# Nine tokens to a partition for k and v, batch 0's q in two transfers, and one batch's q transposed by DMA, in a fused attention and mixer kernel

## The chip, the cores and the metric

The kernel runs on one core of one Trainium2 chip. The metric is the device time of one execution in microseconds (us), start to end. Engines are named as in the profile: PE is TensorE, PEld its weight loads, DVE VectorE, ACT ScalarE, POOL GpSimd, SP the engine that issues most transfers. PEclk is the TensorE clock that was granted, as a share of full speed. The profile is one execution; the times beside it are several executions.

## The reference, cut to what matters

Cosine-reweighted linear attention, then a mixer over tokens with a rank-32 map, then a two-layer MLP, for 8 batches of 576 tokens with 8 heads of 64.

```python
def phi(x, c, s):                      # c, s: cos and sin of pi/2 * pos / 576
    r = np.maximum(x, 0.0)
    return np.concatenate([r * c, r * s], axis=-1)
q_p, k_p = phi(q, cos_w, sin_w), phi(k, cos_w, sin_w)
kv  = einsum('bhsf,bhsd->bhfd', k_p, v)          # 128 x 64 per head
den = einsum('bhsf,bhf->bhs', q_p, k_p.sum(2)) + 1e-6
x   = einsum('bhsf,bhfd->bhsd', q_p, kv) / den   # then heads side by side: 576 x 512
u   = x + (x.transpose(0, 2, 1) @ U @ V).transpose(0, 2, 1)   # U: 576 x 32, V: 32 x 576
out = u + np.maximum(u @ w_ch1, 0.0) @ w_ch2     # 512 -> 2048 -> 512
```

## The kernel before

576 tokens are four times 128 and a rest of 64. The kernel loads four tokens to a partition for 512 of them and the other 64 as a "tail" on 64 partitions; even batches have their tail on partitions 0 to 63, odd ones on 64 to 127. `q_tlT` holds the transposed q tails.

```python
def tail(b):
    lo = TS * (b % 2)                  # TS = 64
    return slice(lo, lo + TS)
...
q_tl = const.tile([P, H, 2 * D], BF16)
q_tlT = const.tile([P, H, P], BF16)
...
def kv_unit(b, hg, tag, bufs, eng=None):         # four heads: 5 matmuls each
    ...
            for c in range(5):
                nc.tensor.matmul(out=acc[:, i, :],
                    lhsT=k_p[b][:, c, h, :] if c < 4 else k_tl[:, h, :],
                    rhs=vx[:, c, h, :], start=(c == 0), stop=(c == 4))
...
def qtr_dma(b, c0, c1):
    ...                                          # c0 = 4: the tail
            nc.sync.dma_start_transpose(
                out=q_tlT[:, :, tail(b)],
                in_=q_tl[tail(b), :, :].rearrange("p h f -> p (h f)"))
...
def qT_of(b, c, h):
    return q_pT[b][:, c, h, :] if c < 4 else q_tlT[:, h, :]
```

The TensorE program is one long row of slots, each a group of MLP matmuls (`g1` is the first layer, `o` the second). The attention of batches 2 to 7 is laid between them at places that a table fixes: the place of kv, then, relative to it, v's and k's and q's preparation, the transposes (`None`: on TensorE; a number: by DMA), `A`, `u`, and the loads of k, v and q of the next batch. Batches 0 and 1 have a hand-written order, since their data has only just been loaded.

```python
ORD = (4, 0, 1, 2, 3)                  # tail first
PLAN = {
    2: (40, (-21, 1, G_), (-14, VV), (-14, VA), None, 14, 17, (-20, -15, -7)),
    3: (58, (-18, 1, A_), (-8, AA), (-13, VA), -11, 15, 18, (-14, 7, 8)),
    ...
}
...
    for n, c in enumerate(ORD if qtr is None else range(5)):
        put(4 + 2 * n, x_unit, c, "X", 1)
```

## Time and profile before

| | before |
|---|---|
| time, median of 3 | 321.14 us (320.8 to 322.12) |
| span in the profile | 319.6 us, clock 1.00 |
| PE, DVE, ACT busy | 97%, 48%, 47% |
| first first-layer matmul | 23.25 us |
| batch 1's kv, whole run | about 36.0 us |
| first tail group of the first layer (`gt`) | 66.82 us |
| batch 2's A | 91.97 us |

The last four rows are places in the program. The lines on which the reading of this kernel rests stand in the prediction below.

### The profile page before, as it was taken

How to read it: one execution, taken by the hardware profiler on the slowest of the kernel's cores; microseconds unless marked ns; L12 is line 12 of the kernel's file. 1: busy time of each engine (PE TensorE's matmuls, PEld its weight loads, DVE VectorE, ACT ScalarE, POOL GpSimd, SP SyncE). 2: the span in 40 equal slices, each digit the busy share in tenths (PEclk: the TensorE clock that was granted, in tenths of full speed). 3: DMA queues.
4: the chain of work that ended last, by engine and by line, in shares of the span. 5: the costliest groups of instructions: out<-in, count | busy, mean ns of one | idle time of the engine just before them, and what ended most of it. 6: DMA issues, size and time to landing. Idle time of an engine off the chain costs nothing.

```text
span 319.6 us, 5754 instructions
## 1 busy us (share of the span) xinstructions
PE 309.3 (97%) x2359; PEld 162.4 (51%) x2386; DVE 154.3 (48%) x341; ACT 150.5 (47%) x251; POOL 34.7 (11%) x71
## 2 busy tenths in 40 slices
PE   8899799999999999999999999999999999999996
PEld 2565464475545544475455444565454444464443
DVE  5866753762777646036926585154836520001211
ACT  3856756685904256658500077558400166750000
POOL 2132500300120140000211100000121100000000
PEclk9999999999999999999999999999999999999999
DMA  7999999999199927990799959940692140001122
GB/s 207 289 267 258 207 192 285 271 266 264 43 199 164 305 89 141 216 283 19 164 194 282 282 117 176 293 126 23 133 212 71 60 98 0 2 0 68 66 83 81
DMA packets 83755, 51.90 MB, mean 162 GB/s; under 512 B 51890, under 2 KB 80946, under 8 KB 83730
## 3 DMA queue, kind: packets, MB, share of 16 engines
q1 hardware_dynamic: 77154, 40.21, 54.2%
q0 software_dynamic: 6432, 11.27, 14.8%
q8 instruction: 18, 0.29, 0.4%
q10 hardware_dynamic: 144, 0.07, 0.1%
q14 instruction: 7, 0.06, 0.1%
HBM read 36.86 MB, written 9.44 MB: 145 GB/s over the span
## 4 chain that ended last, share of the span: by engine, by line
PE 86%; DMA 7%; SPq 2%; ACT 2%; issue 1%; DVE 1%; DVEq 0%
PE o_ps L545 39%; PE g_ps L493 33%; DMA kt<-in_k_dram 5%; PE gt_ps L513 4%; PE kv_ps L271 3%; PE x_ps L365 3%; PE va_ps L409 2%; DMA vst<-in_v_dram 2%; SPq L81 1%; PE a_ps L392 1%; ACT k_p L237 1%; PE t_ps L288 1%; SPq L75 1%; ACT hid L502 0%; PE d_ps L330 0%
## 5 line engine op out<-in xcount | busy, mean ns | idle before, releaser
L502 ACT ACTIVATE hid<-g_ps 128x512 bf16<-128x512 f32 x128 | 76.2, 596 | 101.1 <-PE g_ps L493 100.6
L493 PE MATMUL g_ps<-uT,w_bf 128*128 128x512 bf16 x512 | 118.5, 379 | 0.5 <-DMA w_bf<-in_moe_w_ch_dram 0.4
L545 PE MATMUL o_ps<-w_bf,hid 128*128 128x512 bf16 (+2 forms) x510 | 117.3, 372 | 1.0
L493 PEld LDWEIGHTS <-w_bf 128*128 128x128 bf16 x512 | 48.8, 98 | 56.4 <-issue 0.6
L545 PEld LDWEIGHTS <-hid 128*128 128x128 bf16 x528 | 48.6, 98 | 52.8 <-issue 1.7
L555 DVE TENSOR_TENSOR o_sb<-u_bf,o_ps 128x512 f32<-128x512 bf16 (+2 forms) x33 | 22.1, 669 | 62.7 <-PE o_ps L545 62.6
L565 POOL DMA_DIRECT2D out_dram<-o_sb x24 | 13.5, 564 | 162.6 <-DVE o_sb L555 152.5
L410 DVE TENSOR_TENSOR u_bf<-x_bf,va_ps 128x512 bf16<-128x512 bf16 x32 | 21.8, 686 | 10.1 <-PE va_ps L409 9.7
L105 DVE CAST kv<-kv_ps 128x260 bf16<-128x260 f32 x14 | 6.0, 429 | 32.2 <-PE kv_ps L271 32.2
L237 ACT ACTIVATE q_p<-qst,sinw 128x512 bf16<-128x512 f32 x22 | 15.1, 713 | 5.7 <-DMA qst<-in_q_dram 5.7
L375 DVE TENSOR_TENSOR x_bf<-x_ps,rec 128x512 bf16<-128x512 f32 x24 | 16.6, 692 | 0.8
L513 PE MATMUL gt_ps<-uT_tl,w_bf 128*128 128x128 bf16 x256 | 15.6, 219 | 0.0
L513 PEld LDWEIGHTS <-w_bf 128*128 128x128 bf16 x256 | 14.6, 98 | 0.5
L545 PE MATMUL o_ps<-w_bf,hid_tl 128*128 128x512 bf16 x61 | 14.6, 379 | 0.2
L322 DVE TENSOR_SCALAR rec<-x_ps 128x8 f32<-128x8 f32 (+1 forms) x30 | 5.0, 165 | 20.2 <-PE x_ps L365 20.1
L409 PE MATMUL va_ps<-A_sb,V_bf 128*128 128x512 bf16 x38 | 14.4, 379 | 0.0
L271 PEld LDWEIGHTS <-k_p 128*128 128x128 bf16 x256 | 11.3, 97 | 5.4 <-ACT k_p L237 1.9
L179 PE MATMUL w_ps<-zero 128*128 128x512 bf16 x38 | 12.2, 457 | 1.9 <-DVE halfpi L142 1.2
L271 PE MATMUL kv_ps<-v_ext,k_p 128*128 128x65 bf16 x256 | 12.2, 193 | 1.5 <-ACT k_p L237 0.8
L239 DVE TENSOR_SCALAR k_p<-kst,cosw 128x512 bf16<-128x512 f32 x27 | 12.9, 497 | 0.0
L103 ACT ACTIVATE v_ext<-vst 128x512 bf16<-128x512 f32 (+2 forms) x19 | 12.3, 661 | 1.0 <-DMA vst<-in_v_dram 0.9
L239 DVE TENSOR_SCALAR q_p<-qst,cosw 128x512 bf16<-128x512 f32 x24 | 11.1, 479 | 2.6 <-DMA qst<-in_q_dram 2.6
(105 smaller groups left out, 247.4 us busy)
## 6 DMA issues: line engine op xcount, KB each, us to landing
qst<-in_q_dram SPq DMA_DIRECT2D x8, 1024.0 KB, 10.4
kst<-in_k_dram SPq DMA_DIRECT2D x8, 1024.0 KB, 8.6
vst<-in_v_dram SPq DMA_DIRECT2D x6, 1024.0 KB, 10.6
out_dram<-o_sb POOLq DMA_DIRECT2D x24, 256.0 KB, 4.3
w_bf<-in_moe_w_ch_dram POOLq DMA_DIRECT2D x8, 512.0 KB, 10.9
vst<-in_v_dram SPq DMA_DIRECT2D x4, 512.0 KB, 8.5
out_dram<-o_sb SPq DMA_DIRECT2D x7, 256.0 KB, 2.3
qt<-in_q_dram SPq DMA_DIRECT2D x8, 128.0 KB, 10.4
```

Source lines behind the costliest of these rows:

```text
L237: nc.scalar.activation(out=o, in_=i, func=AF.Relu, bias=0.0, scale=w)
L239: eng.tensor_scalar(out=o, in0=i, scalar1=0.0, scalar2=w, op0=ALU.max, op1=ALU.mult)
L271: nc.tensor.matmul(out=acc[:, i, :], lhsT=k_p[b][:, c, h, :] if c < 4 else k_tl[:, h, :], rhs=vx[:, c, h, :], start=(c == 0), stop=(c == 4),)
L375: nc.vector.tensor_tensor(out=x_of(b, c, rows).rearrange("p (g i d) -> p g i d", g=2, d=D), in0=view[:, :, :, 0:D], in1=rec[rows].unsqueez ...
L409: nc.tensor.matmul(out=va, lhsT=V_bf[:, c, :], rhs=A_sb[b], start=True, stop=True)
L410: nc.vector.tensor_tensor(out=u_bf[b][:, c, :] if c < 4 else u_tl[b // 2][rows, :], in0=x_of(b, c, rows), in1=va[rows, :], op=ALU.add,)
L493: nc.tensor.matmul(out=g_ps.rearrange("p (c t) -> p c t", c=4), lhsT=w1_bf[:, d, j * P : j * P + P], rhs=uT[b][:, :, d, :], start=(d == 0) ...
L502: nc.scalar.activation(out=hid[b][:, j, :], in_=g_ps, func=AF.Relu, bias=0.0, scale=1.0)
L513: nc.tensor.matmul(out=g_ps[:, jj, :], lhsT=w1_bf[:, d, j * P : j * P + P], rhs=uT_tl[pr][:, d, :], start=(d == 0), stop=(d == 3),)
L545: nc.tensor.matmul(out=o[:, cols], lhsT=lhs[:, j, c * P : c * P + P], rhs=w2_bf[:, j, cols], start=(j == 0), stop=(j == NJ - 1),)
L555: nc.vector.tensor_tensor(out=o_sb[:, cols], in0=u[:, cols], in1=o[:, cols], op=ALU.add)
L565: eng.dma_start(out=out[b, 0:512, cols].rearrange("(p c) n -> p c n", c=4)[:, c, :], in_=o_sb[:, cols],)
```

## The change

Its intent is fewer and larger packets and no partial tiles. k and v come with nine consecutive tokens on a partition, so that 64 partitions hold a head and 128 a pair of heads; their tails vanish, and kv becomes 72 matmuls on 64 rows, even and odd head side by side in the two halves of the array. Batch 0's q comes in two transfers ahead of k. Batch 2's q is transposed by DMA as in the later batches.

```diff
+    def load_nine(dst, src, b, g0=0, g1=4, eng=None):
+        (eng or nc.sync).dma_start(
+            out=dst[:, g0:g1, :, :].rearrange("p g c d -> p g (c d)"),
+            in_=src[b].rearrange("(g hh) (p c) d -> (hh p) g (c d)", hh=2, c=9)[:, g0:g1, :],
+        )
...
-    load_main(qst[0], q, 0)
+    load_main(qst[0], q, 0, 0, 4)
+    load_main(qst[0], q, 0, 4, 8)
+    load_nine(kst[0], k, 0)
     load_tail(qt[0], q, 0)
-    load_main(kst[0], k, 0)
-    load_tail(kt[0], k, 0)
...
+        for g in range(g0, g1):
+            for c in range(9):
+                for hh in range(2):
+                    rows = slice(hh * TS, hh * TS + TS)
+                    nc.tensor.matmul(
+                        out=acc[:, hh, (g - g0) * E : (g - g0) * E + E],
+                        lhsT=k_p[b][rows, c, g, :],
+                        rhs=v_ext[b % 2][rows, g, c, :],
+                        start=(c == 0),
+                        stop=(c == 8),
+                    )
...
-            lo = c % 4 * R
+            lo = c % 4 * R if b > 0 else 0        # batch 0's A on 32 rows
...
-        2: (40, (-21, 1, G_), (-14, VV), (-14, VA), None, 14, 17, (-20, -15, -7)),
+        2: (40, (-21, 1, G_), (-14, VV), (-14, VA), -12, 15, 18, (-20, -7, -6)),
...
-        for n, c in enumerate(ORD if qtr is None else range(5)):
-            put(4 + 2 * n, x_unit, c, "X", 1)
+        for c in range(5):
+            put(4 + 2 * c, x_unit, c, "X", 1)
...
     load_main(qst[1], q, 1)
-    load_tail(qt[1], q, 1)
     alloc_k(1)
-    load_main(kst[1], k, 1)
-    load_tail(kt[1], k, 1)
+    load_nine(kst[1], k, 1)
+    load_tail(qt[1], q, 1)
```

What is cut out is above all the hand-written order of batches 0 and 1, rewritten to suit, with 12 matmuls of zeros (they only keep TensorE busy) ahead of batch 0's kv for 13. The changed row of the table also puts batch 2's A and u one place later, and the loads of batch 3's v and q 8 places and 1 place later.

## The prediction

> **What bounds the kernel now.** I read the page's 40 slices first: TensorE (PE) is busy in nearly all of them, VectorE (DVE) and ScalarE (ACT) about half.
>
> ```profile
> PE 309.3 (97%) x2359; PEld 162.4 (51%) x2386; DVE 154.3 (48%) x341; ACT 150.5 (47%) x251; POOL 34.7 (11%) x71
> ...
> PE   8899799999999999999999999999999999999996
> ...
> DMA  7999999999199927990799959940692140001122
> ```
>
> So from about 48 us on only fewer or cheaper matmuls save time. The weak slices are at the start. The chain that ended last, in order of time (start, length, what), says what holds it there:
>
> ```profile
> 7.83 7.97 DMA vst<-in_v_dram
> 15.82 15.75 DMA kt<-in_k_dram
> 31.71 0.64 issue
> ...
> 32.96 1.34 ACT k_p L237 x2
> 34.30 0.48 ACT hid L502
> 34.78 1.24 ACT k_p L237 x2
> 36.06 0.70 PE kv_ps L271 x17
> ```
>
> Batch 0's loads, then the load of batch 1's k tail, then its preparation, then batch 1's kv. TensorE's timeline (start, length, instructions, in brackets its wait) prices those waits, and the units that the change touches:
>
> ```profile
> 23.25 0.60 PE L493 MATMUL g_ps<-uT,w_bf 128*128 128x512 bf16 x2 [0.40 <-DMA w_bf<-in_moe_w_ch_dram]
> ...
> 26.64 0.62 PE L288 MATMUL t_ps<-ident,q_tl 128*128 128x128 bf16 x8 [0.63 <-ACT q_tl L237]
> ...
> 34.78 0.29 PE L271 MATMUL kv_ps<-v_ext,k_p 128*128 128x65 bf16 x2 [0.55 <-POOL v_ext L105]
> 35.45 0.20 PE L271 MATMUL kv_ps<-v_ext,k_p 128*128 128x65 bf16 x1 [0.37 <-ACT k_p L237]
> 36.06 0.20 PE L271 MATMUL kv_ps<-v_ext,k_p 128*128 128x65 bf16 x1 [0.41 <-ACT k_p L237]
> ...
> 69.29 0.61 PE L288 MATMUL t_ps<-ident,q_p 128*128 128x128 bf16 x8 [0.53 <-ACT q_tlT L103]
> ```
>
> After 23.25 us all of TensorE's idle time is under 3 us: that is the most that better loads can give there. The five tail-first transposes of batch 2 (66 to 76 us) are the other visible target. Issue times plus landing times from the DMA view give the queue: batch 1's q lands at 22.6, its q tail at 25.85, k at 30.5, k tail at 31.6, v tail at 32.4.
>
> **What the Trainium skill says.** "TensorE: Matmul & The Clock Gate", Part 3, says matmuls on different row groups run together and weight loads overlap running matmuls only when the row group differs. No row pair runs in this trace, but the A unit's four column tiles do: four 128x256 matmuls of 283 ns take 0.29 us together, so they start a few ns apart. "TensorEngine Tiling (Array Packing)", Key Properties, says a change of tiling mode drains the array. The trace agrees:
>
> ```profile
> 90.80 1.24 PE L545 MATMUL o_ps<-w_bf,hid_tl 128*128 128x512 bf16 x5
> ...
> 91.97 0.40 PE L392 MATMUL a_ps<-x_bf,U_bf 128*32 128x512 bf16 x4
> 92.19 0.38 PE L392 MATMUL a_ps<-x_tl,U_bf 128*32 128x512 bf16 x1
> ...
> 92.51 1.04 PE L545 MATMUL o_ps<-w_bf,hid_tl 128*128 128x512 bf16 x4
> ```
>
> At the 0.216 us spacing of 512-column matmuls the first A matmul could start at 91.88 and the next output matmul at 92.41; both come about 0.1 us late. The two 32-row matmuls that spread V show the same 0.09 us at each end. "DMA: Bandwidth & Descriptors", Queues, rings and completion order, says each DMA engine drains a ring in order and alternates between rings packet by packet. The landing times agree: q's tail is only 512 packets of 256 B, yet lands 3.2 us behind q while the first-layer weights (other queue) are loading.
>
> **The change part by part.**
>
> *Loads.* In the packet records of 16 to 36 us a 256 B packet takes 26 ns of an engine, 1 KB 58, 2304 B 124 (only V's load), a weight packet 96. An engine's share of k or v is 64 x 58 + 32 x 26 = 4.5 us before, 32 x 124 = 4.0 after: about half a microsecond each.
>
> *Batch 0.* First data moves at 3.3 us; q's first half should land at about 5.2, the second at 7.0, k at 10.9 (k with tail 12.0 before). K preparation becomes 18 operations of 256 columns for 10 of 512. A DVE one now comes every 0.40 us; at an estimated 0.26 the eleven on DVE take 2.9 us, so kv starts near 14.2 (14.74 before). But kv then takes 36 matmuls for 20 in each half, with four mode changes, so the first layer starts only about 0.3 us earlier, near 22.9.
>
> *Batch 1.* Here I expect a loss. Its q tail now queues behind all of k. DVE, ACT and TensorE take it first (tail-first order is kept, and all three run in program order). One engine's work from the end of batch 0's loads (15.6 us) to that tail: q 64 x 58 + k 32 x 124 + tail 32 x 26 + two weight loads 64 x 96 = 14.7 us, so it lands near 30 instead of 25.85. The same sum for the kernel before (q, q tail, k, k tail and the weights: 15.2 us from 16.4, where V and U have landed) gives 31.6 for its k tail; the profile has 31.57. TensorE would then stand at the tail's transposes from 26 to 30.6. After it DVE still has five q cosines, two sines, five evacuations and nine k cosines: 7 x 0.40 + 5 x 0.65 + 9 x 0.26 = 8.4 us, so the full kv run starts at 38.4 for 36.0: +2.4 us. The waits on k and v before kv vanish, but they are inside the 36.0.
>
> *kv elsewhere.* 72 half-height matmuls for 40 full ones. A full one costs 30 ns here (20 in 0.61 us); the denominators' one-column matmuls, 25 ns apart, show that weight loads go no slower than that. With perfect pairs 36 x 30 = 1.1 us, with serial weight loads 72 x 25 = 1.8, against 1.2. I take 1.37. With two mode changes (0.19) that is +0.35 for each of batches 2 to 7, +2.1; in batch 1, in two pieces, +0.5.
>
> *Batch 0's A.* It now lies on 32 rows, so its 5 u products, 4 uT-tail products and last uT pair become 32-row matmuls among 128-row ones: 10 places, 2 changes each, at 0.095 us: +1.9.
>
> *Batch 2's transposes.* 40 off TensorE at 56 ns (the chain has 0.45 for eight) is -2.2, and the 0.53 us wait goes. DMA replaces them: three transposes with medians of 3.5 to 5.1 us, sent 12 places before the plan's origin while the consumer comes 4 after it; they should be hidden although DMA is full then.
>
> Sum: +2.4 + 0.5 + 2.1 + 1.9 - 2.7 = +4.2, so about 325.3 us.
>
> **The rivals.**
>
> *The start gets better.* If the q tail lands by 27.5, or something else holds DVE less, batch 1's kv starts 1 to 2 us before 36.0, and with perfect pairs the sum is near -2: 319. For it: removing tails visibly aims at the longest link of the chain, and the code around it has been adjusted as a tuned version would be. Against it: the queue sum met three landings of the kernel before within a microsecond.
>
> *Weight loads serialise in kv.* Then +0.8 instead of +0.35 per batch, another +3: 328. For it: full-height loads at 25 ns spacing; against it: the skill's sentence on row groups.
>
> *Clock loss.* "TensorE: Matmul & The Clock Gate", Part 1, says an idle window of about 3.4 us halves the clock. No wait before is long enough to show it; a 4.6 us stand at 26 us might, for an estimated 2 us more.
>
> *Late DMA transposes.* k, v and q of batches 2 and 3 share the rings in 50 to 72 us. If batch 2's transposes slip behind them, the 2.7 us go back.
>
> **Range and chances.** The sum is 325.3, the friendly rival 319. The batch 1 term is the largest and rests on a queue model, so I set the number between, nearer the sum: 323.3 us, with 318.0 to 328.8 for 8 times in 10. Steady work holds TensorE at 97% and only 2.7 us of it is removed, so more than 2% faster (below 314.7) has 0.03. More than 2% slower (above 327.6) needs the batch 1 loss and a second rival: 0.17. Within 2%: 0.80.
>
> **What the profile after would show.** Right, if q's tail of batch 1 lands near 30 us; TensorE waits 3 us or more before the q_tl transposes; the first-layer matmuls start near 22.9; kv's 72 matmuls take 1.1 to 1.8 us; gaps of 0.1 us stand on both sides of batch 0's va matmuls; nothing waits for batch 2's q_pT. Wrong, if that wait is under 1.5 us and batch 1's kv runs before 36 us: then the time is below 321. A kv of 2 us or more, or a clock below full in the slices at 25 to 35 us, would put it above my range.

## The result

The changed kernel takes 335.96 us (335.67 to 337.35, 4 runs) where the kernel before takes 321.36 us (320.8 to 322.12, 4 runs in the same rounds). Executions over 1.5% slower than the fastest of the same kernel are left out of the means. Ratios are computed from the mean time of one kernel's runs over that of the other's runs of the same rounds, so they are not quite the ratio of the medians: here 1.0461, with a 95% interval of 1.0424 to 1.0498. It is 4.6% slower, outside the predicted range.

The page of the profile after, first its busy sums, then slices of 8.4 us each:

```profile
PE 314.9 (94%) x2572; PEld 163.6 (49%) x2596; DVE 156.1 (47%) x376; ACT 149.0 (44%) x268; POOL 34.7 (10%) x71
...
PE   8699999999728999999999999999999999999996
...
PEclk9859999999996999999999999999999999999999
DMA  7996999449990694797099768980297150001122
```

PE is 5.6 us busier than before, but the span grew by 15.6 us. There are two holes. The second slice is thin on PE and the third low in clock; the eleventh and twelfth (84 to 101 us) show PE at 7 and 2 tenths, and the clock is low after them. Before, PE had 9 there and a full clock throughout. The same program places in both kernels, from TensorE's timeline:

| place (us) | before | after | difference added in the stretch |
|---|---|---|---|
| first first-layer matmul | 23.25 | 26.76 | +3.51 |
| first `gt` matmul | 66.82 | 70.67 | +0.34 |
| A of batch 2 | 91.97 | 107.15 | +11.33 |
| last group of `gt` | 281.73 | 297.07 | +0.16 |
| end of the last PE instruction | 316.59 | 331.93 | 0.00 |

So 11.3 of 15.3 us arise between 71 and 107 us, at batch 2, and 3.85 before 71 us. (The kernel before does batch 2's tail transposes, 0.45 us, just ahead of its first `gt`; the changed kernel has none there, so without them the start costs 4.3 us.) The long rest, where kv of five batches was expected to cost more, gives almost nothing.

**The start.** The chain that ended last, after (start, length, what), in answer to the chain at 7.83 us and later of before:

```profile
1.80 8.87 DMA kst<-in_k_dram
10.69 2.30 DVE k_p L230 x8
13.06 0.87 DVE k_p L230 x3
13.93 0.67 DVE v_ext L111
```

k lands at 10.67 us, its preparation and v's hold DVE to 14.6 us. kv starts at 14.74 us, exactly as before. What changed is TensorE's state. Its timeline after (start, length, instructions, in brackets its wait):

```profile
14.74 1.18 PE L265 MATMUL kv_ps<-v_ext,k_p 64*128 64x65 bf16 x36 [3.24 <-DVE v_ext L111]
...
79.72 1.33 PE L265 MATMUL kv_ps<-v_ext,k_p 64*128 64x65 bf16 x72
```

With q in two transfers ahead of k, and its tail's transposes moved behind kv, the other transposes and the 12 matmuls of zeros were done by 11.5 us; TensorE then stood for 3.24 us. Before, the zeros ended just as kv began. The windows view of the changed kernel, 14 to 26 us (window, length, then busy time with count of PE, PEld, DVE, ACT, POOL, then clock, DMA share, GB/s):

```profile
14.00:26.00 12.00, 11.15 (x183) 8.51 (x184) 6.42 (x18) 4.04 (x9) 2.83 (x7) 0.57 1.14 283
```

Before, the clock in the same window was 1.00. Here it was 0.50 until about 24.6 us, so batch 0's attention ran at half speed. "TensorE: Matmul & The Clock Gate", Part 1, in the Trainium skill, says that an idle window of about 3.4 us halves the clock and that the window runs free. Here the clock fell at 14.4 us, 2.9 us after the last matmul of zeros, and in e5 below a stand of 1.93 us was enough: by these measurements the window need not be idle in full.

**Batch 2.** SP issues the loads of q, k and v and the transposes in program order. Its timeline of the kernel before, 68 to 95 us (start, length, line, operation):

```profile
68.29 0.37 SPq L75 DMA_DIRECT2D qst<-in_q_dram  x1
...
86.94 6.18 SPq L301 DMA_TRANSPOSE q_pT<-q_p  x2
93.22 1.69 SPq L306 DMA_TRANSPOSE q_tlT<-q_tl  x1
```

and of the kernel after:

```profile
70.80 4.22 SPq L299 DMA_TRANSPOSE q_pT<-q_p  x2
75.11 1.91 SPq L304 DMA_TRANSPOSE q_tlT<-q_tl  x1
...
78.97 0.81 SPq L81 DMA_DIRECT2D qst<-in_q_dram  x1
...
92.78 5.31 SPq L299 DMA_TRANSPOSE q_pT<-q_p  x2
98.13 2.15 SPq L304 DMA_TRANSPOSE q_tlT<-q_tl  x1
```

The load of batch 3's q (`qst`) stands in line behind the new transposes of batch 2 and goes out at 79.0 instead of 68.3 us. So batch 3's own transposes go out at 92.8 and 98.1 instead of 86.9 and 93.2 us. That by itself need not hurt: batch 3's x is not due yet. But TensorE's timeline after shows who waits:

```profile
89.51 0.42 PE L363 MATMUL x_ps<-kv,q_pT 128*128 128x65 bf16 x8 [1.79 <-DVE x_bf L373]
93.73 0.43 PE L363 MATMUL x_ps<-kv,q_pT 128*128 128x65 bf16 x8 [2.08 <-DVE x_bf L373]
102.02 0.62 PE L363 MATMUL x_ps<-kv,q_tlT 128*128 128x65 bf16 x8 [6.13 <-DMA q_tlT<-q_tl]
```

The last of these is the tail unit of batch **2**'s x, and it waits for the tail transpose of batch **3**. The chain shows the whole path:

```profile
78.97 9.67 DMA qst<-in_q_dram
...
91.86 1.93 ACT q_p L228 x3
93.79 3.99 ACT k_p L228 x10
97.78 0.31 SPq L299
...
98.13 3.84 DMA q_tlT<-q_tl
102.02 0.62 PE x_ps L363 x8
102.65 4.57 PE o_ps L552 x12
```

A reading of the code explains it. `q_tlT` is one tile, an even batch's tail in one half and an odd batch's in the other, and x reads all of it. With the transposes on TensorE batch 2 took its tail first (`ORD`), at place 40 + 4 = 44. With DMA transposes the order is 0 to 4, so that the tail comes last, at 40 + 12 = 52. Batch 3's tail transpose has place 58 - 11 + 4 = 51. It is one place earlier in the program, so batch 2's last reader comes after it and must wait for it, although batch 2's own tail has been there since about 80 us. In the other pairs the reader comes first: 98 + 12 = 110 against 126 - 12 + 4 = 118, and 165 + 12 = 177 against 197 - 10 + 4 = 191.

The three waits in brackets are 10.0 us together. The half clock after the last of them costs an estimated 2.3 us more: from x's tail unit to A the changed kernel takes 5.13 us (102.02 to 107.15), where 12 output matmuls at 0.216 us and a unit of x at 0.26 us would take 2.85.

### The profile page after: what moved, and what is told of

Read it like the earlier page. It is cut to its first block, busy times and chain, and to the rows that moved or that the text cites. A ratio compares the mean times of both kernels' runs of the same rounds, so it can differ in the third digit from the quotient of the medians.

```text
span 335.2 us, 6228 instructions
## 1 busy us (share of the span) xinstructions
PE 314.9 (94%) x2572; PEld 163.6 (49%) x2596; DVE 156.1 (47%) x376; ACT 149.0 (44%) x268; POOL 34.7 (10%) x71
## 4 chain that ended last, share of the span: by engine, by line
PE 81%; DMA 7%; DVE 4%; ACT 3%; issue 2%; SPq 2%; ACTq 0%; DVEq 0%
PE g_ps L500 33%; PE o_ps L552 31%; PE gt_ps L520 4%; PE kv_ps L265 3%; DMA qst<-in_q_dram 3%; DMA kst<-in_k_dram 3%; PE va_ps L416 2%; PE x_ps L363 2%; DVE k_p L230 2%; ACT k_p L228 2%; PE a_ps L390 2%; DMA q_tlT<-q_tl 1%; PE xh_ps L345 1%; DVE u_bf L417 1%; PE t_ps L286 1%
## 5 line engine op out<-in xcount | busy, mean ns | idle before, releaser
L230 DVE TENSOR_SCALAR k_p<-kst,cosw 128x256 bf16<-128x256 f32 x59 | 19.4, 353 | 1.7 <-DMA kst<-in_k_dram 1.7
L109 ACT ACTIVATE v_ext<-vst 128x576 bf16<-128x576 f32 x21 | 13.5, 676 | 11.0 <-DMA vst<-in_v_dram 11.0
L111 DVE CAST kv<-kv_ps 128x520 bf16<-128x520 f32 (+1 forms) x8 | 5.1, 632 | 28.5 <-PE kv_ps L265 28.5
L228 ACT ACTIVATE q_p<-qst,sinw 128x512 bf16<-128x512 f32 (+1 forms) x24 | 15.1, 657 | 4.2 <-DMA qst<-in_q_dram 2.3
L552 PE MATMUL o_ps<-w_bf,hid_tl 128*128 128x512 bf16 x62 | 16.5, 418 | 0.2 <-issue 0.2
L265 PE MATMUL kv_ps<-v_ext,k_p 64*128 64x65 bf16 x576 | 12.7, 197 | 3.4 <-DVE v_ext L111 3.2
L520 PE MATMUL gt_ps<-uT_tl,w_bf 128*128 128x128 bf16 x256 | 15.6, 219 | 0.0
L228 ACT ACTIVATE k_p<-kst,sinw 128x256 bf16<-128x256 f32 x34 | 15.2, 494 | 0.9 <-DMA kst<-in_k_dram 0.9
L520 PEld LDWEIGHTS <-w_bf 128*128 128x128 bf16 x256 | 14.6, 98 | 0.9 <-issue 0.2
L265 PEld LDWEIGHTS <-k_p 64*128 64x128 bf16 x576 | 11.4, 98 | 7.1 <-ACT v_ext L109 3.7
L230 DVE TENSOR_SCALAR q_p<-qst,cosw 128x512 bf16<-128x512 f32 (+1 forms) x28 | 12.2, 456 | 3.7 <-DMA qst<-in_q_dram 3.6
L363 PE MATMUL x_ps<-kv,q_pT 128*128 128x65 bf16 x192 | 10.1, 194 | 3.9 <-DVE x_bf L373 3.9
```

Of the source, the lines that this page charges most:

```text
L228: nc.scalar.activation(out=o, in_=i, func=AF.Relu, bias=0.0, scale=w)
L230: eng.tensor_scalar(out=o, in0=i, scalar1=0.0, scalar2=w, op0=ALU.max, op1=ALU.mult)
L265: nc.tensor.matmul(out=acc[:, hh, (g - g0) * E : (g - g0) * E + E], lhsT=k_p[b][rows, c, g, :], rhs=v_ext[b % 2][rows, g, c, :], start=(c ...
L363: nc.tensor.matmul(out=acc[:, g, i * E : i * E + E], lhsT=qT_of(b, c, h), rhs=kv_sb[b][:, h, :], start=True, stop=True,)
L520: nc.tensor.matmul(out=g_ps[:, jj, :], lhsT=w1_bf[:, d, j * P : j * P + P], rhs=uT_tl[pr][:, d, :], start=(d == 0), stop=(d == 3),)
L552: nc.tensor.matmul(out=o[:, cols], lhsT=lhs[:, j, c * P : c * P + P], rhs=w2_bf[:, j, cols], start=(j == 0), stop=(j == NJ - 1),)
```

## The experiments

All kernels were correct. All were timed beside the kernel before in the same rounds; its medians there were 320.4, 320.67, 320.35, 320.82 and 320.61 us in the five groups. "Stretch" below is the time from the first `gt` matmul to batch 2's A in the profile: 25.15 us before, 36.48 us after. The change moves A one place later, four output matmuls of 0.216 us, so a kernel with A at the later place and nothing else should have 26.0. The stretch of the kernel before holds four of batch 2's five transposes (1.8 us) and the 0.53 us wait before one of them.

### e1_warm and e5_warm_qt_first: the gap at the start

```diff
-    keep_warm(12, "o", 2)
+    keep_warm(27, "o", 2)
```

> Edit: 27 warm-up matmuls in place of 12 before batch 0's kv, nothing else. Theory: the 3.24 us in which TensorE stood before kv halved its clock from 14.7 to 24.7 us; with the gap filled the clock stays full and the first first-layer matmuls start near 23.3 us in place of 26.76. But batch 1's q tail lands only at 27.9, so TensorE then waits 3 to 4 us before the q_tl transposes and batch 1's kv starts at most 1 us earlier: total 334.5 to 335.5. Rival: the clock loss is on the path to the end in full, total near 332.5.

The changed kernel with more matmuls of zeros took 335.61 us (334.72 to 336.7; ratio to before 1.0467). The clock was full to 40 us and the first first-layer matmul came at 25.24 us instead of 26.76, but batch 1's kv came at 37.37 us, only 0.25 us sooner. TensorE now waited 0.83 us for batch 1's q tail, a wait that its lateness had hidden. Later, from 40 to 44 us, the clock fell to 0.57 in this execution. In this profile the first `gt` came 1.4 us later than without the edit (72.08 for 70.67 us), so the later dip took back more than the filled gap gave. The gap at the start is thus not what makes most of the loss; what it costs alone is asked again in g1.

e5 had the same zeros and batch 1's q tail loaded ahead of its k.

```diff
     load_main(qst[1], q, 1)
+    load_tail(qt[1], q, 1)
     alloc_k(1)
     load_nine(kst[1], k, 1)
-    load_tail(qt[1], q, 1)
```

> Edit: 27 warm-up matmuls, and batch 1's q tail loaded before k in place of after it. Theory: q tail lands near 24.5, no wait at the q_tl transposes, batch 1's kv starts near 34.5 in place of 37.6, total about 332. Rival (the order of these loads does not matter, k is what batch 1 waits for): the same as with the warm-ups alone.

It took 336.22 us (ratio 1.0501), a miss. The q tail landed at 22.8 us as intended, but TensorE stood 1.93 us at the matmuls that spread V, with no releaser in the profile, the clock was 0.50 from about 22.3 to 25.7 us, and batch 1's kv came at 38.69 us. The run says nothing on the q tail; i2 below asks again.

### e2_two_tails and e3_pe_transpose: batch 2 in the changed kernel

e2 gives even and odd batches a tail tile each.

```diff
-    q_tlT = const.tile([P, H, P], BF16)
+    q_tlT2 = [const.tile([P, H, P], BF16, name=f"q_tlT{i}") for i in range(2)]
...
-        return q_pT[b][:, c, h, :] if c < 4 else q_tlT[:, h, :]
+        return q_pT[b][:, c, h, :] if c < 4 else q_tlT2[b % 2][:, h, :]
```

> Edit: q_tlT gets two buffers, one for even and one for odd batches, nothing else. Theory: batch 2's last x unit reads both halves of the shared tile, so it waits for batch 3's tail transpose; with its own tile the 6.1 us wait goes, and with it the half clock from 100 to 106 us (about 2.6 us): total 326 to 328. Rival: batch 3's late loads (v at 86, q at 88.6) are the limit in themselves, the wait moves to batch 3's kv or x units, and the total stays above 332.

It took 329.89 us (327.02 to 330.23; ratio 1.0275). The 6.13 us wait was gone, of the two others 1.00 us was left, and the stretch fell from 36.48 to 24.97 us. The theory's 326 to 328 was met by the profiled run alone; the other three had a mean clock of 0.974 to 0.979 against its 0.984. The rival, above 332, is out.

e3 puts batch 2's transposes back on TensorE, with x tail first.

```diff
-        2: (40, (-21, 1, G_), (-14, VV), (-14, VA), -12, 15, 18, (-20, -7, -6)),
+        2: (40, (-21, 1, G_), (-14, VV), (-14, VA), None, 15, 18, (-20, -7, -6)),
...
+        if qtr is None:
+            for n, c in enumerate(ORD):
+                put(-9 + 2 * n, qtr_unit, c, 0, H, A_ if n % 2 == 0 else V_)
```

> Edit: batch 2's q transposed on TensorE again, tail first, as in the kernel before; all else as in the changed kernel. Theory: the DMA transposes hold up batch 3's v and q loads in the same queue and bring the false wait with them; without them the waits between 85 and 107 us (10 us, and 2.6 us of half clock) go and 2.2 to 2.7 us of transposes come back: total 325 to 326.5. Rival: v and q of batch 3 are late because the plan asks for them late (7 and 6 slots before, for 15 and 7): then waits stay there and the total is above 330.

It took 330.36 us (328.95 to 332.25; ratio 1.0313). The stretch was 25.73 us, so batch 2 cost nothing any more, as the theory said, but the time was 4 us above its range. The time lies in the rival's range (above 330), but the waits that the rival expected did not stay. What is left of the loss is not at batch 2: in the profile the start is later still (first `gt` at 71.62 us), and the times go with a clock of 0.974 to 0.984.

### e4_packed_a: batch 0's A

```diff
-            lo = c % 4 * R if b > 0 else 0
+            lo = c % 4 * R
...
-        return V_bf if b > 0 else V_32
+        return V_bf
```

> Edit, on the changed kernel: only A of batch 0 packed on 128 rows again, so that its 11 products are no 32-row matmuls. Theory: 0.1 us per change of tiling mode, about 20 of them, 1.5 to 1.9 us less: 334.1 to 334.5, and no gaps around the va matmuls. Rival: 32-row products cost nothing: 335.5 to 336.5.

It took 334.43 us (333.68 to 335.72; ratio 1.0443 against the change's 1.0461, from other rounds). By these the part costs between 0.6 and 1.5 us, not distinguishable from nothing with confidence. The trace is clearer. From the first `uTt` matmul to the end of the eight u products the changed kernel takes 10.54 us (54.95 to 65.49); e4 takes 9.09 us (57.17 to 66.26), and so do g2 below, also with A packed (54.39 to 63.48), and the kernel before. (In these last two the record of one u product is missing; its time is there.) Each u product on 32 rows stands 1.29 us from the next instead of 1.08.

### f1, f2 and g4: the transposes alone, on the kernel before

f1 changes one line of the kernel before.

```diff
-        2: (40, (-21, 1, G_), (-14, VV), (-14, VA), None, 14, 17, (-20, -15, -7)),
+        2: (40, (-21, 1, G_), (-14, VV), (-14, VA), -12, 15, 18, (-20, -15, -7)),
```

> Edit, on the kernel BEFORE: only batch 2's q transposed by DMA, with the plan numbers of the changed kernel; token layout, loads and batch 0 as before. Theory: this part alone brings most of the loss, because the tail's transpose of batch 3 now comes ahead of batch 2's last x unit on a tile that both use: TensorE waits 5 to 8 us at that unit and loses up to 2 us of clock, against 2.7 us saved, total 324 to 328. Rival (the part is a gain on its own and only the late loads of the changed kernel spoil it): 317.5 to 319.

It took 330.44 us (328.78 to 332.28; ratio 1.0319): this part alone costs 10 us, more than the theory gave it. TensorE's timeline shows waits of the same kinds as in the changed kernel, on x's evacuation and on the tail:

```profile
87.42 0.43 PE L365 MATMUL x_ps<-kv,q_pT 128*128 128x65 bf16 x8 [2.79 <-DVE x_bf L375]
96.42 0.62 PE L365 MATMUL x_ps<-kv,q_tlT 128*128 128x65 bf16 x8 [6.84 <-DMA q_tlT<-q_tl]
```

and the stretch was 35.60 us. The load of batch 3's q went out at 75.77 us here, with its place in the plan unchanged: so 7.5 us of delay come from the transposes ahead of it on SP. In the changed kernel it went out at 79.0 us; that kernel is itself 3.85 us late by then and has v's load in the same line.

f2 is f1 with two tail tiles, by the edit of e2:

```diff
-    q_tlT = const.tile([P, H, P], BF16)
+    q_tlT2 = [const.tile([P, H, P], BF16, name=f"q_tlT{i}") for i in range(2)]
```

> Edit, on the kernel BEFORE: batch 2's q transposed by DMA, and two q_tlT tiles. Theory: with the shared tile gone the 2.7 us come through but for a short wait on batch 3's q, which is loaded behind the transposes: 317.5 to 320. Rival: the late q of batch 3 still stops VectorE and so TensorE for 3 us or more: above 321.

It took 320.3 us (318.83 to 321.49; ratio 0.9995, 0.9955 to 1.0036), with a stretch of 24.75 us. All 10 us went with the sharing.

g4 is f1 with one tile, but with batch 2's tail taken first.

```diff
-        for n, c in enumerate(ORD if qtr is None else range(5)):
+        for n, c in enumerate(ORD if b == 2 else range(5)):
```

> The kernel before with batch 2's q transposed by DMA and one tail tile, but batch 2's x taken tail first, so that its last reader of the shared tail tile comes in the program ahead of batch 3's tail transpose. Theory: the 6.8 us wait goes although the tile is shared, and the time is 319.5 to 322 us, as with two tiles. Rival: the wait comes from the transpose's own slowness and moves to another unit: 328 to 331.

It took 319.82 us (317.96 to 320.3; ratio 0.9959, 0.9899 to 1.0018), with a stretch of 24.95 us. The tile is still shared, batch 3's q still goes out late, at 75.0 us; only the reader's place moved ahead of the writer's. This settles the mechanism: the false dependency is made by the order in the program.

### f3 and g2: the changed kernel with everything mended

f3 has the two tail tiles of e2 and the packed A of e4, and besides:

```diff
-        2: (40, (-21, 1, G_), (-14, VV), (-14, VA), -12, 15, 18, (-20, -7, -6)),
+        2: (40, (-21, 1, G_), (-14, VV), (-18, VA), -15, 15, 18, (-20, -15, -10)),
-    keep_warm(12, "o", 2)
+    keep_warm(22, "o", 2)
```

> Edit, on the changed kernel: 22 warm-ups, two q_tlT tiles, A of batch 0 packed on 128 rows again, batch 2's q prepared and transposed 3 to 4 places earlier and batch 3's v and q loaded 8 and 4 places earlier. Theory: waits at batch 2 and the mode changes of batch 0's A go; what is left against the kernel before is the later start of batch 1: about 322. Rival (the nine-token layout itself costs more than the model says): above 325.

It took 324.82 us (322.92 to 325.48; ratio 1.0129), between theory and rival. Nothing waits at batch 2 (stretch 23.71 us), but TensorE still stood 2.47 us before kv, the clock was low from 18 to 28 us and again from 41 to 45 us.

g2 is f3 with 31 matmuls of zeros.

```diff
-    keep_warm(22, "o", 2)
+    keep_warm(31, "o", 2)
```

> The kernel with everything mended, with 31 matmuls of zeros instead of 22, so that none of the wait for batch 0's kv is left. Theory: its remaining 4 us over the kernel before are the clock at the start and batch 1's wait: the clock stays full to 36 us, the first first-layer matmul comes at about 25.5 us, and the time is 322 to 323.5 us, still above the kernel before because batch 1's q tail and k preparation set the place at 38 us. Rival: the low clock costs nothing here because batch 1's data is awaited anyway; the time stays at 324.8.

It took 324.35 us (322.22 to 325.22; ratio 1.0103, 1.0048 to 1.0159). The profiled run had a full clock to 72 us and beyond (mean 0.999) and was the fastest, 322.22; the others had 0.984 to 0.995. The half microsecond to f3 is inside the scatter. The rival is not excluded.

### g1_before_gap: the gap alone, on the kernel before

```diff
-    keep_warm(13, "o", 2)
```

> The kernel before without the thirteen matmuls of zeros ahead of batch 0's kv, nothing else: TensorE then stands about 3.7 us, from 11.0 to 14.7 us. Theory: the granted clock falls to 0.5 for some ten microseconds, the first first-layer matmul comes at 26 to 27 us instead of 23.25, and the kernel takes 322.5 to 324.5 us; part of the 3.5 us comes back as shorter waits for batch 1's loads. Rival: the lower clock of the changed kernel has another cause (the half-height matmuls), the clock stays at 1.0 here and the time stays at 320.7.

The windows view of this kernel, columns as above:

```profile
14.00:26.00 12.00, 11.09 (x160) 7.69 (x163) 6.56 (x19) 5.10 (x10) 2.84 (x7) 0.72 1.16 268
26.00:40.00 14.00, 12.71 (x124) 7.59 (x124) 10.30 (x22) 10.68 (x18) 6.44 (x9) 0.92 1.19 232
```

A wait of 3.49 us took the clock to 0.50 from 14 to about 21 us, and it dipped again near 39 us. The fall is as the theory said, though for 7 us and not ten, and it came with full-height matmuls, so half-height ones are not its cause. The first first-layer matmul came at 24.53 us, 1.3 us late. The time was 320.12 us (319.95 to 322.45; ratio 0.9998, 0.9945 to 1.0051): the theory's cost did not come. Batch 1's kv stood at 34.71 us, as before (34.78), because it waits for batch 1's data anyway. The profiled execution was the slowest of the four, 322.45 us: its first `gt` came at 68.36 us for 66.82, after the second dip. The other three, with mean clocks of 0.989 to 0.995, took 319.95 to 320.17 us.

### g3, h1, i1: is there a gain in the transposes at all?

g3 is f2 with q's preparation and transposes, and batch 3's q load, earlier, and with A and u back in their places.

```diff
-        2: (40, (-21, 1, G_), (-14, VV), (-14, VA), -12, 15, 18, (-20, -15, -7)),
+        2: (40, (-21, 1, G_), (-14, VV), (-18, VA), -15, 14, 17, (-20, -15, -10)),
```

> The kernel before, batch 2's q transposed by DMA, two tail tiles, and batch 2's q preparation and transposes four and three places earlier, with batch 3's q load three places earlier; A one place earlier again. Theory: with no wait left at batch 2, the 2.2 us of transposes that TensorE saves and the 0.5 us wait come out: 317.5 to 319 us against 320.7. Rival: the transposes delay other transfers by as much: 320 to 321.

It took 320.89 us (ratio 1.0006, 0.9962 to 1.005). The stretch was 22.68 us, 2.5 less than before, but ahead of it, at 63.31 us, TensorE waited 2.06 us for ACT, whose q preparation now stood among the evacuations of the first layer.

h1 is g4 with A back in its place and batch 3's q load three places earlier.

```diff
-        2: (40, (-21, 1, G_), (-14, VV), (-14, VA), -12, 15, 18, (-20, -15, -7)),
+        2: (40, (-21, 1, G_), (-14, VV), (-14, VA), -12, 14, 17, (-20, -15, -10)),
```

> The kernel before with batch 2's q transposed by DMA, its x tail first, A one place earlier again and batch 3's q loaded three places earlier. Theory: the 1.2 us wait on x's evacuation goes and the saved transposes come through: 318 to 319 us, about 0.6% below the kernel before. Rival: the gain is lost in the scatter or given back elsewhere: within 0.3% of the kernel before.

It took 323.62 us (321.61 to 324.75; ratio 1.0086, 1.0052 to 1.012), about 0.9% slower, clear of the scatter. The wait on x's evacuation was gone and a new one stood at batch 2's own tail, with a clock of 0.50 from 80.3 to 87.1 us:

```profile
82.03 0.62 PE L365 MATMUL x_ps<-kv,q_tlT 128*128 128x65 bf16 x8 [3.80 <-DMA q_tlT<-q_tl]
```

SP's timeline of h1 gives the likely reason: the load of q now stands ahead of the tail's transpose, and its 1.1 MB share the rings with it. The transpose landed 6.9 us after its issue; in g4, where it goes ahead of the loads, such transposes took at most 3.9 us.

```profile
74.34 0.62 SPq L75 DMA_DIRECT2D qst<-in_q_dram  x1
75.06 1.54 SPq L306 DMA_TRANSPOSE q_tlT<-q_tl  x1
```

i1 is g4 with A back in its place and the loads where they were.

```diff
-        2: (40, (-21, 1, G_), (-14, VV), (-14, VA), -12, 15, 18, (-20, -15, -7)),
+        2: (40, (-21, 1, G_), (-14, VV), (-14, VA), -12, 14, 17, (-20, -15, -7)),
```

> The kernel before with batch 2's q transposed by DMA, x tail first, A and u where the kernel before has them, and every load where it was. Theory: the TensorE time saved comes through but for the 1.2 us wait on x's evacuation: 318 to 319.3 us, 0.5 to 0.9% below the kernel before. Rival: within 0.3% of the kernel before.

It took 319.72 us (319.41 to 321.03) against 320.61 for the kernel before (ratio 0.998, 0.9951 to 1.0008). The stretch was 22.96 us, 2.2 less than before with no wait in it; the four transposes in the stretch and their wait were 2.3 us. The fifth, 0.45 us, lies ahead of the stretch and is saved as well. In time the gain is 0.9 us by medians and not distinguishable from none (the clock dipped to 0.60 in 36 to 40 us of the profiled run). No version that was run beats the kernel before beyond doubt.

### h2_after_tail_first: the order alone, in the changed kernel

```diff
-        for c in range(5):
-            put(4 + 2 * c, x_unit, c, "X", 1)
+        for n, c in enumerate(ORD if b == 2 else range(5)):
+            put(4 + 2 * n, x_unit, c, "X", 1)
```

> The changed kernel with only the order of batch 2's x changed to tail first. Theory: the 6.1 us wait on the tail's transpose goes, as with two tiles: 329 to 331 us. Rival: q of batch 3 still lands late and holds everything, so that the wait moves to the next unit: above 333 us.

It took 328.25 us (326.12 to 330.76; ratio 1.0249, 1.0203 to 1.0295), with a stretch of 25.57 us. Against the changed kernel's own rounds that is 7.7 us by medians, from the order of five units.

### h3 and i2: the nine-token layout alone

h3 is the changed kernel with batch 2 as in the kernel before (transposes as in e3), A packed as in e4, and 31 matmuls of zeros.

```diff
-        2: (40, (-21, 1, G_), (-14, VV), (-14, VA), -12, 15, 18, (-20, -7, -6)),
+        2: (40, (-21, 1, G_), (-14, VV), (-14, VA), None, 14, 17, (-20, -15, -7)),
-    keep_warm(12, "o", 2)
+    keep_warm(31, "o", 2)
```

> The nine-token layout of k and v alone: q of batch 2 transposed on TensorE, its plan and loads as in the kernel before, batch 0's A on four column tiles, 31 matmuls of zeros so that the clock stays full. Theory: the layout itself costs little, mostly through batch 1's later q tail and 0.2 us a batch for kv: 322 to 324 us. Rival: the layout is neutral once the clock is kept up: 320 to 321.5 us.

It took 326.15 us (325.99 to 326.61; ratio 1.0174, 1.0145 to 1.0203), above both expectations. Its stretch was 24.86 us, its first `gt` at 70.58 us, 3.8 us late, and that is where its loss lies. TensorE stood 1.36 us at 20.83 us with no releaser, the zeros ended later than kv's data came (kv at 16.64 us), and the clock fell to 0.64 in 24 to 28 us.

i2 is h3 with batch 1's q tail loaded ahead of k, as in e5, and 25 zeros.

```diff
     load_main(qst[1], q, 1)
+    load_tail(qt[1], q, 1)
     alloc_k(1)
     load_nine(kst[1], k, 1)
-    load_tail(qt[1], q, 1)
-    keep_warm(31, "o", 2)
+    keep_warm(25, "o", 2)
```

> The nine-token layout alone, as in the run before, but with batch 1's q tail loaded ahead of its k, and 25 matmuls of zeros for 31. Theory: the layout's cost comes from the q tail standing behind k: batch 1's kv starts before 36.8 us and the time falls from 326 to 322 to 323.5 us. Rival: it comes from elsewhere (k preparation in 18 pieces, stalls, the clock): above 325 us.

The profiled run took 322.24 us with a clock of 0.998; its start was better than that of the kernel before. The chain that ended last in it, at batch 1:

```profile
33.58 1.21 ACT k_p L228 x3
34.83 0.51 PE kv_ps L265 x20
```

The last uninterrupted kv run stands at 34.8 us for 36.0 before, and the first `gt` at 66.11 us for 66.82. But one other run took 326.29 us, and four took 327.15 to 327.85 us, with clocks of 0.978 to 0.983: all five lie in the range of the rival. The median of all six is 327.29 us; the ratio of the two fast runs is 1.0113, 1.0049 to 1.0177. The order of the loads can make the layout's start good; what spoils it in most executions is not shown, since their profiles were not taken.

## Why the prediction was wrong

**The reading of the bound held.** TensorE's time and its waits are the time of this kernel; from 120 us on the two kernels run alike.

**The step that failed** is the sentence on batch 2's transposes: "they should be hidden although DMA is full then", with the term -2.7. In the place of -2.7 the stretch at batch 2 grew by 11.3 us, and that part alone, on the kernel before, cost 10 us in time (f1). I had priced what the transposes take off TensorE and asked when their own consumer comes. I had not asked two other things: which transfers stand behind them in SP's line (batch 3's q, 7.5 us later in f1), and who else reads or writes their destination. The rival "late DMA transposes" named the shared rings, but its worst case was that the 2.7 us go back. That nothing waits for batch 2's `q_pT` was right and did not help; the wait was at `q_tlT`, for another batch's data. Undone by two tiles (f2) or by the order alone (g4, h2), it goes. The size that I gave the saving was right: 2.2 us less stretch in i1 and 0.45 us ahead of it, of which the timed runs do not show more than 0.9. In time, mending batch 2 in the changed kernel brings 5.6 to 7.7 us by medians (e3, e2, h2), from other rounds, less than the 11 us of the stretch.

**Batch 0** was predicted at kv near 14.2 and the first layer near 22.9 us. k landed at 10.67 for 10.9, and kv came at 14.74: DVE's eleven operations took 3.2 us for 2.9, with a v cast after them. The first layer came at 26.76 us, because the 3.24 us wait before kv halved the clock. I looked for a clock loss at 26 us and not here, where fewer zeros and an earlier q open the gap. It cost less than it looks: g1 has it on the kernel before and loses nothing measurable in time, because batch 1's data sets the next date there, and e1 fills it and gains nothing in time, though there a later dip of the clock hides what it is worth.

**Batch 1** was +2.4 us, with the last kv run at 38.4 us for 36.0. The number came out nearly right, in part by luck. The chain at batch 1 after, to be held against the last line of the prediction's chain (36.06 us):

```profile
37.62 1.11 PE kv_ps L265 x16
...
38.75 0.51 PE kv_ps L265 x20
```

The first 16 matmuls go at the pace of k's preparation; the uninterrupted run begins at 38.75 us: +2.7. (37.62 us is the first kv matmul, for 34.78 before: +2.8.) The last of k's pieces on DVE ends at 38.60 us, so the path through DVE that I named is there. But the start of that path was wrong. The q tail landed at 27.9 us (issued at 15.0, 12.9 us to landing) and not near 30; k's packets took 104 ns each and not the 124 that V's gave, which moreover stand at 14 to 15.4 us, outside the window that I named for them. The 3 us wait before the q tail's transposes did not show, because TensorE, late from the half clock, came to them only at 29.56 us; with a full clock it is 1.21 us (g2). The tail's place in the queue has the support of i2's profile, where the tail ahead of k brings the last kv run to 34.8 us, but the timed runs of i2 leave its worth open.

**Batch 0's A on 32 rows** was +1.9. The trace has 1.45 us of it in one row of `uTt` and u products; the remaining places lie in the batch 1 chain, where they cannot be told apart. From batch 1's last kv run to the first `uTt` the changed kernel takes 16.20 us (38.75 to 54.95) for 16.00 (36.06 to 52.06); those 0.2 us hold these and what was left of the +0.5 for kv in two pieces. Together the terms for the start, predicted +4.5, came to 4.3 us (3.85 with the 0.45 us of batch 2's tail transposes taken off): 2.7, 0.2 and 1.45.

**kv elsewhere** was +0.35 a batch. From batch 2's A to the last `gt` both differ by 0.16 us; with 0.86 us for the later place of A the five batches in it cost 1.02, 0.2 each. 72 matmuls took 1.33 us, near the 1.37 that I took, so the rival of serial weight loads is out; only the changes of mode cost less. The sentence that the prediction quotes against that rival, that weight loads overlap running matmuls only when the row group differs, does not fit the kernel before in its "only": from 303 to 310 us its full-height matmuls keep PE busy for 6.95 of 7 us, while 33 full-height weight loads take 3.23 us of the same time.

**What stays open.** With batch 2 mended and nothing else the changed kernel is still 8 to 10 us slower in time (h2 1.0249, e2 1.0275, e3 1.0313), of which the start gives about 4 to 5 in the profiles. With A packed and more zeros as well the nine-token kernels are 3.3 to 5.6 us slower (g2 1.0103, h3 1.0174), while their profiles at best reach the kernel before (i2). Runs of one kernel go with the clock: in e2 327.02 us at 0.984 and 330.2 us at 0.974. Which short waits lower it in which execution was not settled; in i1 it was 0.50 from 36.8 to 40.2 us after several waits, none longer than 0.72 us.

## What to carry to other kernels

When a transfer is added, look at what it delays in its issuing engine's line and at every other reader and writer of the tile it fills; a tile shared by halves is one tile to the order of the program, and an old reader that stood one place behind the new writer cost nearly 8 us here (h2). Move a producer off a busy engine only after writing down the program places of the last old reader and the next writer. A wait that makes a striking line, here a clock at half speed for ten microseconds, costs only what the next fixed date does not absorb: test it alone before mending it.

## What the Trainium skill lacked or had wrong

- "TensorE: Matmul & The Clock Gate", Part 1, gives about 3.4 us of sustained activity for the clock to come back, and an idle window of the same length for it to fall. In the changed kernel it stayed at 0.50 from 14.4 to about 24.6 us while PE was busy for 7.88 of 8 us (16 to 24 us, with ends that the profile models), and in g1 for about 7 us. In e5 it fell after a stand of 1.93 us, in i1 after none above 0.72 us.
- The same page, in its account of the 56 ns gap, says that starts of matmuls are never less than about 25 ns apart, and names no exception there. On two row groups 72 matmuls of 65 columns took 1.33 us, 18.5 ns each on average.
- "TensorEngine Tiling (Array Packing)", Key Properties, says that a change of mode drains the array and gives no figure. One 32-row matmul of 512 columns between full-height ones cost 0.21 us more than a full-height one (1.29 for 1.08 us), two changes.
- "DMA: Bandwidth & Descriptors", DMA Transpose (X-bar), gives constraints but no time for a small transpose (the page has a bandwidth elsewhere). The 64-row tail transposes in the changed kernel hold SP for 1.4 to 2.2 us each and land 3.0 to 4.9 us after issue, and loads placed behind batch 2's three went out 7.5 us later (f1).
- No page was found that tells of stands of TensorE without a releaser at the start (0.71 us in e1, 1.93 in e5, 1.36 in h3). The nearest, "Runtime: NRT & Kernel Launch", Instruction fetch mechanics, has stalls of the fetch for taken branches alone. The runs do not show the cause: a transfer of the instruction queue ran from 19.7 to 20.7 us in e5, into the stand, but in h3 it ended as the stand began (20.8 us) and in e1 0.9 us before it.
